# Linear attention in plain float32 on parts of TensorE, its keys and queries in bursts beside the feed-forward

## The chip, the cores and the metric

The kernel runs on one core of a Trainium2 chip. The time is that of one execution on the device in microseconds (us), lower is better. The core has a matrix engine (PE, which loads weights, PEld, and streams a moving operand against them), a vector engine (DVE), an activation engine (ACT), GpSimd (POOL), and a queue of transfers that SyncE (SP) issues. Each takes its own instructions in order; semaphores join them. Matmul results land in PSUM, eight banks of 2 KB per partition, and DVE or ACT must read a bank before it can be used again.

## The reference

Eight batches of eight heads, 576 tokens, head dimension 64, 128 features; then a feed-forward of 512 to 2048 to 512 over all 4608 tokens:

```python
def phi(x):
    proj = np.einsum('bhsd,df->bhsf', x, w_phi)
    proj = proj - np.max(np.abs(proj), axis=-1, keepdims=True)
    return np.concatenate([np.exp(proj), np.exp(-proj)], axis=-1)
q_p, k_p = (phi(q), phi(k))
kv = np.einsum('bhsf,bhsd->bhfd', k_p, v)
z = np.sum(k_p, axis=2)
num = np.einsum('bhsf,bhfd->bhsd', q_p, kv)
den = np.einsum('bhsf,bhf->bhs', q_p, z)[..., None] + 1e-06
x = num / den                      # heads side by side: 4608 x 512
h = x @ w_in
g = h * np.tanh(softplus(h))
out = g @ w_out
```

The weights of the feed-forward come as float64 and are brought to float32 on the chip. All else is float32.

## The kernel before

The feed-forward works on 18 chunks of 256 tokens. For each chunk `ff_in` (L352) makes 16 blocks of 128 hidden features, 12 matmuls of 128x128 by 256 columns each; `mish` (L367) applies the activation to two blocks; `ff_out` (L384) adds 6 matmuls of 512 columns a block into two PSUM tiles `o`. Both use float32r, a faster form of float32 on PE: every operand is a sum of a high and a low part (`gh` and `gl`, `xTh` and `xTl`, the two halves of a weight tile), and three products stand for one. `split_weight` (L116) turns 32 pieces of float64 words into such parts, with four operations on DVE, three on ACT and two on POOL a piece.

The keys are 72 units of 256 columns. `k_proj` (L203) calls `project` (L149): ACT and POOL split the raw keys, six float32r matmuls against a w_phi that holds two heads side by side give `pp_k`, DVE takes the largest magnitude (`m_k`, L146) and subtracts it (`d_k`, L165), ACT takes the two exponentials. `k_sum` (L210) adds `kvps` with the values stationary (66 columns: 64 values, a column of ones for the denominator, and one of zeros) and the 256 features as the moving operand, in plain float32. The result lies the wrong way round, is turned by `kvt` (L230), and goes out to DRAM and back.

A query unit is two heads of one chunk; there are four a chunk. `q_proj` (L252) splits and projects (`pp_q`, L177), `q_turn` (L256) transposes the result (`dt_q`), `q_exp` (L266) takes exponentials, once in float32 and once in float32r with the low part by POOL, `q_num` (L301) makes numerator and denominator in three float32r products with `kvs`, a split copy of kv; `q_den` (L326) sends the denominators through DRAM to spread them over the partitions, `q_out` (L340) divides.

The order comes from a table of due times (L405 to L456) in units of one feed-forward block: every call gets a time, they are sorted, and the framework's scheduler then places the instructions on the engines. All 72 key units have times below zero (`t0`, L429), 1.1 units apart, ahead of the first block; the query units of a chunk are four blocks apart during the chunk before. Weight pieces are spread over the same stretch.

Of the kernel before, what the change touches and what calls it, by code (L numbers as in the profile page):

```python
# [8 lines left out]
F32 = mybir.dt.float32  # L9
# [7 lines left out]
P = 128  # L17
# [4 lines left out]
VW = D + 2  # L22
# [5 lines left out]
NRAW, NE, NEH, NEL, NV, NKV = 3, 4, 2, 2, 2, 5  # L28
NHALF, NX, NRB, NXT, NG = 2, 2, 1, 3, 4

GP, GQ, GV = 2.2, 2.2, 1.5
GK, VLOAD = 2.7, 1.5
LOAD, WLOAD, KVLOAD = 4.0, 3.0, 3.0
Q0, Q1, QOUT, QL = -1.0, 4.0, 4.5, 0.5
QPOS, UPRE = 60, 1.1
W0, W1 = 4.0, 2.0
LAG, TAIL, TAILLAG = 4, 10, 2

KPLAIN, QPLAIN = 1, 1

NSPARE, WIN, MSPARE = 32, 4, 5
# [3 lines left out]
def attention_then_mish(ctx, tc, qT, kT, va, w_phi, w_in, w_out, out):  # L45
# [5 lines left out]
    dram = ctx.enter_context(tc.tile_pool(name="dram", bufs=4, space=bass.MemoryType.DRAM))  # L51
# [13 lines left out]
    def raw_tile(name):  # L65
        return work.tile([P, 2, 2 * P], F32, tag="raw", name=name, bufs=NRAW)

    def half_tile(name):
        return work.tile([P, 512], F32, tag="half", name=name, bufs=NHALF)


    wphi_raw = moe.tile([P, 2 * F], F32, tag="xTh", name="wphi_raw", bufs=NXT)
    nc.sync.dma_start(wphi_raw, w_phi[0])
    wphi_hi = moe.tile([P, 2 * F], F32R, tag="gh", name="wphi_hi", bufs=NG)
    wphi_lo = moe.tile([P, 2 * F], F32R, tag="gl", name="wphi_lo", bufs=NG)
    nc.vector.tensor_copy(wphi_hi, wphi_raw)
    nc.vector.tensor_sub(wphi_lo, wphi_raw, wphi_hi.bitcast(F32))
    wst_raw = moe.tile([P, 2 * F], F32, tag="xTl", name="wst_raw", bufs=NXT)
    nc.sync.dma_start(wst_raw, w_phi[1])
    wst = const.tile([P, 2 * F], F32R, tag="wst", name="wst")  # L80
    nc.vector.tensor_copy(wst, wst_raw)
    nc.vector.tensor_sub(wst[:D, F:], wst_raw[:D, F:], wst[:D, F:].bitcast(F32))
# [7 lines left out]
    spare = [f"w{kind}_{i}_{j}" for kind, i, j in pieces[-NSPARE:]]  # L90
    turn = 0
# [5 lines left out]
    def pair_tile(name):  # L97
        nonlocal turn
        if len(spare) >= MSPARE:
            turn += 1  # L100
            return slot_tile(spare[turn % min(WIN, len(spare))], F32, name)
        return work.tile([P, 2, 512], F32, tag="e", name=name, bufs=NE)

    piece = 0

    def load_weight(kind, i, j):
        nm = f"{kind}_{i}_{j}"
        if f"w{nm}" in spare:
            spare.remove(f"w{nm}")
        src = w_in[i * P:(i + 1) * P, j * 512:(j + 1) * 512] if kind == "in" else w_out[i * P:(i + 1) * P, :]  # L110
        slot = f"w{kind}_{i}_{j}"
        words = slot_tile(slot, U32, f"words_{nm}").rearrange("p a b -> p (a b)")
        nc.sync.dma_start(words, src.bitcast(U32))
        weight[kind, i, j] = words.rearrange("p (a b) -> p a b", b=2)

    def split_weight(kind, i, j):  # L116

        nonlocal piece
        nm = f"{kind}_{i}_{j}"
        slot = f"w{kind}_{i}_{j}"  # L120
        words = weight[kind, i, j]
        low, high = words[:, :, 0], words[:, :, 1]
        tag, bufs = ("u", 3) if piece % 5 < 3 else ("ee", 2)
        piece += 1
        w = moe.tile([P, 512], U32, tag=tag, name=f"w_{nm}", bufs=bufs)
        scale = moe.tile([P, 512], U32, tag="n", name=f"scale_{nm}")
# [9 lines left out]
        parts = slot_tile(slot, F32R, slot)  # L136
# [5 lines left out]
    def less_max(d, name):  # L142

        d3 = d.rearrange("p (n f) -> p n f", f=F)
        m = work.tile([P, 4], F32, tag="m", name=f"m_{name}", bufs=3)
        nc.vector.tensor_reduce(m, d3, axis=AX.X, op=ALU.max, apply_absolute_value=True)  # L146
        return d3, m.unsqueeze(2).broadcast_to([P, 4, F])

    def project(raw, plain, name):  # L149

        parts = ((raw, wphi_raw),)
        if not plain:
            hl = work.tile([P, 2, 2 * P], F32R, tag="hl", name=f"hl_{name}")
            hi, lo = hl[:, 0, :], hl[:, 1, :]
            nc.scalar.copy(hi, raw)  # L155
            nc.gpsimd.tensor_sub(lo, raw, hi.bitcast(F32))  # L156
            parts = ((hi, wphi_hi), (hi, wphi_lo), (lo, wphi_hi))
        ps = (ps_h if starting else ps_att).tile([P, 512], F32, tag="h" if starting else "att", name=f"pp_{name}")
        for i in range(2):
            for k, (x, w) in enumerate(parts):  # L160
                nc.tensor.matmul(ps[:, i * 2 * F:(i + 1) * 2 * F], x[:, i * P:(i + 1) * P], w,  # L161
                                 start=(k == 0), stop=(k == len(parts) - 1))
        d = pair_tile(f"d_{name}")
        p3, m = less_max(ps, name)
        nc.vector.tensor_tensor(d[:, 0, :].rearrange("p (n f) -> p n f", f=F), p3, m, op=ALU.subtract)  # L165
        return d

    def project_stacked(raw, name):

        x = work.tile([P, 2, 2 * P], F32R, tag="hl", name=f"hl_{name}")  # L170
        nc.scalar.copy(x, raw)  # L171
        nc.gpsimd.tensor_sub(x[D:], raw[D:], x[D:].bitcast(F32))  # L172
        d = pair_tile(f"d_{name}")
        for i in range(2):
            ps = ps_att.tile([P, 2, 2, F], F32, tag="att", name=f"pp{i}_{name}")
            for j in range(2):
                nc.tensor.matmul(ps[:, j], x[:, j, i * P:(i + 1) * P], wst, start=True, stop=True)  # L177
            di = d[:, 0, i * 2 * F:(i + 1) * 2 * F].rearrange("p (j f) -> p j f", f=F)
            nc.scalar.copy(di, ps[:, :, 1, :])
            nc.vector.tensor_tensor(di, ps[:, :, 0, :], di, op=ALU.add)  # L180
        d3, m = less_max(d[:, 0, :], name)
        nc.vector.tensor_tensor(d3, d3, m, op=ALU.subtract)
        return d


    kv, kv_dram = {}, {}
    k_live, k_raw, v_live, kv_ps = {}, {}, {}, {}

    def k_load(b, u):
        n = 9 * b + u  # L190
        if n % 2 == 0:
            k_raw[n // 2] = raw_tile(f"kraw_{n // 2}")
            nc.sync.dma_start(k_raw[n // 2], kT[n // 2])
        k_live[b, u] = k_raw[n // 2][:, n % 2, :]

    def v_load(b, u):
        for pair, first in ((0, 0), (1, 4), (2, 9), (3, 13)):
            if first // 2 == u:
                vt = work.tile([P, 5, 2, VW], F32, tag="v", name=f"v_{b}_{pair}", bufs=NV)
                nc.sync.dma_start(vt.rearrange("p t j w -> p (t j w)"), va[b * NHP + pair])  # L200
                v_live[b, pair] = vt

    def k_proj(b, u):  # L203
        nm = f"k_{b}_{u}"
        e = project(k_live.pop((b, u)), 9 * b + u < KPLAIN, nm)
        nc.scalar.activation(e[:, 1, :], e[:, 0, :], AF.Exp)
        nc.scalar.activation(e[:, 0, :], e[:, 0, :], AF.Exp, scale=-1.0)  # L207
        k_live[b, u] = e

    def k_sum(b, u):  # L210
        e = k_live.pop((b, u))
        for i in range(2):
            t = 2 * u + i
            for pair, first in ((0, 0), (1, 4), (2, 9), (3, 13)):
                slot = t - first
                if not 0 <= slot < 5:
                    continue
                if slot == 0:
                    pool, tag = (ps_o, "o") if starting else (ps_att, "att")
                    kv_ps[pair] = pool.tile([P, 2, 2, F], F32, tag=tag, name=f"kvps_{b}_{pair}")  # L220
                vt = v_live[b, pair]
                for j in range(2):
                    nc.tensor.matmul(kv_ps[pair][:VW, j], vt[:, slot, j, :], e[:, :, (2 * i + j) * F:(2 * i + j + 1) * F],  # L223
                                     start=(slot == 0 and j == 0), stop=(slot == 4), skip_group_check=True)
                if slot == 4:
                    kvT = half_tile(f"kvT_{b}_{pair}")
                    nc.scalar.copy(kvT[:VW], kv_ps.pop(pair)[:VW].rearrange("w j s f -> w (j s f)"))
                    ps = ps_att.tile([P, 512], F32, tag="att", name=f"kvt_{b}_{pair}")
                    for n in range(4):
                        nc.tensor.transpose(ps[:, n * VW:(n + 1) * VW], kvT[:VW, n * P:(n + 1) * P], ident[:VW, :VW])  # L230
                    t2 = work.tile([P, 4 * VW], F32, tag="kv", name=f"kvo_{b}_{pair}", bufs=NKV)
                    nc.vector.tensor_copy(t2, ps[:, :4 * VW])
                    kv_dram[b, pair] = dram.tile([P, 4 * VW], F32, tag=f"kvd_{b}_{pair}", name=f"kvd_{b}_{pair}", bufs=1)
                    nc.sync.dma_start(kv_dram[b, pair], t2)
                    del v_live[b, pair]
# [261 lines left out]
```

## Time and profile before

| what | value |
|---|---|
| median of 3 runs | 1229.3 us (1227.18 to 1231.24) |
| the profiled execution, its own time | 1229.93 us |
| its span | 1228.0 us |
| mean granted clock of PE | 0.996 |
| instructions | 21711, of them 8094 matmuls |
| HBM read, written | 69.40 MB, 13.91 MB |

The page gives busy times, and groups of instructions with "busy, mean ns of one | idle before". A matmul's own length holds its way through the array and is longer than its pitch, the distance from one start to the next, by which a row of them advances. The chain of waits, followed back from the last instruction, gives pitches: there a piece "x12" is the time in which twelve matmuls went by. The table by stage gives each engine's busy time in stretches of the span. The lines themselves stand in the prediction, beside the sums made from them.

### The profile page before, as it was taken

To read this page: it belongs to the slowest core of one execution; us is meant where nothing else is said; L and a number is where in the kernel's file an instruction comes from. 1 tells how busy PE (TensorE), PEld (TensorE's weight loads), DVE (VectorE), ACT (ScalarE), POOL (GpSimd) and SP (SyncE) were. 2 spreads that over 40 slices of the span, in tenths; PEclk is the share of its full clock that TensorE was granted. 3 is DMA by queue.
4 is the path that set the end of the run, shared out by engine and by line. 5 is a ranking of instruction groups with operands and counts; after the bars stand their busy time and mean duration, and the time that the engine had idled before them with its cause. 6 is when DMAs were issued, how large, how long until landed. Compare 5 with 4: busy or idle time off the path is not lost.

```text
span 1228.0 us, 21711 instructions
## 1 busy us (share of the span) xinstructions
PE 1199.2 (98%) x8094; PEld 1064.4 (87%) x8094; DVE 597.2 (49%) x987; ACT 895.2 (73%) x1704; POOL 594.9 (48%) x509
## 2 busy tenths in 40 slices
PE   8999998899999999999999999999999999999998
PEld 6776776688999899999999999999999999999997
DVE  6987887954443344334443444334343444344211
ACT  6887877788777767777777777777777777777531
POOL 3765665856544545454444544545454544544200
PEclk9999999899999999999999999999999999999999
DMA  5665657311111211110121111111111111010000
GB/s 194 206 187 176 200 159 229 99 57 36 53 44 40 61 31 51 38 53 27 49 65 36 44 28 56 31 53 27 57 61 32 44 40 53 27 36 14 25 24 18
DMA packets 62025, 84.87 MB, mean 69 GB/s; under 512 B 17632, under 2 KB 35808, under 8 KB 61920
## 3 DMA queue, kind: packets, MB, share of 16 engines
q1 hardware_dynamic: 61920, 83.49, 22.0%
q8 instruction: 63, 1.03, 0.3%
q14 instruction: 42, 0.34, 0.1%
HBM read 69.40 MB, written 13.91 MB: 68 GB/s over the span
## 4 chain that ended last, share of the span: by engine, by line
PE 81%; DVE 7%; DMA 5%; ACT 2%; issue 2%; POOL 1%; SPq 0%; POOLq 0%; DVEq 0%
PE h L364 33%; PE o L395 32%; PE num_q L313 8%; PE kvps L223 3%; PE pp_q L177 2%; PE dt_q L262 2%; DMA words_out<-w_out 2%; DMA words_in<-w_in 2%; DVE m_k L146 1%; DVE d_k L165 1%; PE pp_k L161 1%; DVE scale_in L133 1%; DVE scale_out L128 1%; DMA rb<-r 1%; DVE w_in L132 1%
## 5 line engine op out<-in xcount | busy, mean ns | idle before, releaser
L364 PE MATMUL h<-xTh,win 128*128 128x256 f32 x2304 | 466.3, 284 | 0.0
L381 DVE TENSOR_TENSOR gl<-u,gh 128x256 fp32r<-128x256 f32 x288 | 169.1, 613 | 479.6 <-ACT gh L380 476.5
L364 PEld LDWEIGHTS h<-xTh,win 128*128 128x128 f32 x2304 | 378.2, 190 | 9.4
L395 PE MATMUL o<-wout,gh 128*128 128x512 f32 x1152 | 364.5, 396 | 0.0
L364 PE MATMUL h<-xTl,win 128*128 128x256 f32 x1152 | 325.3, 283 | 0.0
L279 POOL TENSOR_TENSOR el_q<-d_q,eh_q 128x512 fp32r<-128x512 f32 x136 | 180.0, 1335 | 295.4 <-ACT eh_q L278 295.4
L364 PEld LDWEIGHTS h<-xTl,win 128*128 128x128 f32 x1152 | 219.0, 190 | 6.8
L395 PE MATMUL o<-wout,gl 128*128 128x512 f32 x576 | 224.8, 391 | 0.0
L395 PEld LDWEIGHTS o<-wout,gh 128*128 128x128 f32 x1152 | 198.4, 189 | 25.8
L223 PE MATMUL kvps<-d_k,v 128*66 128x256 f32 x640 | 151.9, 383 | 5.4 <-ACT d_k L207 4.4
L172 POOL TENSOR_TENSOR hl_q<-qraw,hl_q 64x512 fp32r<-64x512 f32 x68 | 88.5, 1301 | 105.5 <-ACT hl_q L171 90.2
L272 ACT ACTIVATE d_q<-dt_q 128x512 f32<-128x512 f32 x144 | 86.1, 601 | 71.6 <-PE dt_q L262 71.3
L395 PEld LDWEIGHTS o<-wout,gl 128*128 128x128 f32 x576 | 108.3, 188 | 23.8
L223 PEld LDWEIGHTS kvps<-d_k,v 128*66 128x66 f32 x640 | 86.0, 139 | 48.2 <-ACT d_k L207 6.7
L380 ACT CAST gh<-u 128x256 fp32r<-128x256 f32 x288 | 109.0, 406 | 20.5 <-PE o L395 11.9
L372 ACT ACTIVATE u<-h 128x512 f32<-128x512 f32 x144 | 86.1, 598 | 49.7 <-PE h L364 49.0
L313 PE MATMUL num_q<-eh_q,kvs 128*66 128x256 f32 (+3 forms) x736 | 107.9, 255 | 0.9 <-ACT eh_q L278 0.9
L298 POOL TENSOR_TENSOR kvs<-kv,kvs 128x264 fp32r<-128x264 f32 x92 | 81.4, 895 | 19.3 <-ACT kvs L297 13.7
L313 PE MATMUL num_q<-el_q,kvs 128*66 128x256 f32 (+3 forms) x368 | 88.9, 256 | 1.2 <-POOL el_q L279 1.2
L372 ACT ACT_TABLE_LOAD x69 | 88.5, 1283 | 1.2
L156 POOL TENSOR_TENSOR hl_k<-kraw,hl_k 128x256 fp32r<-128x256 f32 x71 | 60.5, 856 | 57.8 <-ACT hl_k L155 57.7
L161 PE MATMUL pp_k<-wphi_hi,hl_k 128*128 128x256 f32 x284 | 76.3, 331 | 10.9 <-DVE d_k L165 9.8
(74 smaller groups left out, 1694.9 us busy)
## 6 DMA issues: line engine op xcount, KB each, us to landing
qraw<-qT SPq DMA_DIRECT2D x136, 128.0 KB, 3.0
v<-va SPq DMA_DIRECT2D x32, 330.0 KB, 3.4
kraw<-kT SPq DMA_DIRECT2D x36, 256.0 KB, 3.5
rb<-r SPq DMA_DIRECT2D x72, 128.0 KB, 3.0
out<-osb SPq DMA_DIRECT2D x36, 256.0 KB, 2.1
words_in<-w_in SPq DMA_DIRECT2D x16, 512.0 KB, 4.4
words_out<-w_out SPq DMA_DIRECT2D x16, 512.0 KB, 4.1
kvd<-kvo SPq DMA_DIRECT2D x32, 132.0 KB, 1.8
```

Of the source, the lines that this page charges most:

```text
L161: nc.tensor.matmul(ps[:, i * 2 * F:(i + 1) * 2 * F], x[:, i * P:(i + 1) * P], w, start=(k == 0), stop=(k == len(parts) - 1))
L172: nc.gpsimd.tensor_sub(x[D:], raw[D:], x[D:].bitcast(F32))
L223: nc.tensor.matmul(kv_ps[pair][:VW, j], vt[:, slot, j, :], e[:, :, (2 * i + j) * F:(2 * i + j + 1) * F], start=(slot == 0 and j == 0), sto ...
L272: nc.scalar.activation(e, ps, AF.Exp, scale=2.0 * s - 1.0)
L279: nc.gpsimd.tensor_sub(el, e, eh.bitcast(F32))
L298: nc.gpsimd.tensor_sub(wl, w, wh.bitcast(F32))
L313: nc.tensor.matmul(ps[:VW, j, r0:r1], w[:, j, s, :], e[:, j * CH + r0:j * CH + r1], start=first, stop=(s == 1 and k == len(parts) - 1), sk ...
L364: nc.tensor.matmul(ps, w[:, wcol], x[:, cc % 2, :], start=(n == 0), stop=(n == 11))
L372: nc.scalar.activation(u, hv, AF.Mish)
L380: nc.scalar.copy(gh, u[:, f * CH:(f + 1) * CH])
L381: nc.vector.tensor_sub(gl, u[:, f * CH:(f + 1) * CH], gh.bitcast(F32))
L395: nc.tensor.matmul(ps, g[:, cols], w, start=(i == 0 and k == 0), stop=(i == NFT - 1 and k == 2))
```

## The change

The attention is in plain float32 throughout, and its matmuls use parts of the array.

- **Projections.** The raw tile has head j of a pair on partitions 64j to 64j+63. `project` (new L113) issues, for each 128 tokens, one matmul on rows 0 to 63 and one on rows 64 to 127, each of 128 features, into two different PSUM tiles. There are 576 of them, for keys and queries alike; nothing is split.
- **Sums.** In `halves` (new L133) phi is the stationary operand, 64 of its columns at a time, and the output goes to the matching half of the PSUM partitions; the moving operand is the 66 columns of the values, or of kv. Keys: 1280 such matmuls of 64 columns by 66; queries: 1152. kv comes out the right way round and stays in SBUF (`NKV` = 10 tiles); the 64-column halves also let one tile of queries straddle two batches.
- **Division.** The denominator now lies along partitions beside its numerator: DVE adds 1e-6, takes the reciprocal of 128x4 and multiplies (new L217 to L219). `x` is then transposed by PE (`xt`, new L227).
- **Order.** 36 key steps of 512 columns and 36 query steps (half a chunk, four heads) go together, key step n with query step n - 5 (`LEAD`). The first steps stand 2.4 units apart, the others 8, so that most keys fall beside the feed-forward. In each step the two projections stand together, and the exponentials come in two bursts of four. `table` (new L105) ties all exponentials and Mish calls into one order on ACT.

```diff
-NRAW, NE, NEH, NEL, NV, NKV = 3, 4, 2, 2, 2, 5
+NRAW, NE, NV, NKV = 4, 6, 3, 10
...
+NK, LEAD, USTART = B * NHP * S // 512, 5, 2.4
+E0, E1, GX = 0.27, 0.36, 1.2
...
+    def project(raw, name):
...
+        for n in range(4):
             for j in range(2):
+                rows = slice(j * D, (j + 1) * D)
+                nc.tensor.matmul(ps[j][:, n], raw[rows, n * P:(n + 1) * P], w_phi2[rows], start=True, stop=True)
...
+    def halves(ps, lhsT, rhs, start, stop):
+
+        for h in range(2):
+            rows = slice(h * D, (h + 1) * D)
+            nc.tensor.matmul(ps[rows], lhsT[:, rows], rhs[h], start=start, stop=stop, skip_group_check=True)
...
+                for j in range(2):
+                    for s in range(2):
+                        halves(ps[:, j, s], es[j][:, s, i * P:(i + 1) * P], (vt[:, slot, j, :],) * 2,
+                               start=(slot == j == s == 0), stop=(slot == 4))
...
+        for i in range(2):
+            ps = ps_att.tile([P, 2, 2, VW], F32, tag="att", name=f"num{i}_{c}_{g}")
+            for t in range(2):
+                r0 = (2 * c + t) * P
                 for j in range(2):
+                    for s in range(2):
+                        halves(ps[:, t, j], es[j][:, s, (2 * i + t) * P:(2 * i + t + 1) * P],
+                               [kv[(r0 + h * D) // S, 2 * g + i][:, j, s] for h in range(2)],
+                               start=(t == j == s == 0), stop=(s == 1))
...
+    steps = [(n - LEAD, n if n < NK else None, divmod(n - LEAD, 2) if 0 <= n - LEAD < 2 * NCH else None)
+             for n in range(LEAD + 2 * NCH)]
+    when = {n: 8.0 * n - 18.0 if n >= 2 else 8.0 * 2 - 18.0 - USTART * (2 - n) for n in range(-LEAD, 2 * NCH + 1)}
+    for n, key, query in steps:
+        t, t1 = when[n], when[n + 1]
+        d = t1 - t
...
+            at(t, k_proj, key)
...
+            at(t + 0.03, q_proj, *query)
...
+            at(t1 + 0.01, k_sum, key)
...
+            at(t1 + 0.02, q_num, *query)
+            at(t1 + GX, q_out, *query)
```

Two places show how the order changes. The first is DVE where the first low part of an activation (`gl` of chunk 0) is made, the mark of the feed-forward's start. Before, 326 instructions stand ahead of it, the last key unit (`m_k_8`, `d_k_8`) among them:

```order
L165 TENSOR_TENSOR d_k_7_2589<-pp_k_7_2582,m_k_7_2590 128x512
L232 COPY kvo_1_2572<-kvt_1_2567 128x264
L128 TENSOR_SCALAR scale_out_0_2790<-words_out_0_2707 128x512
L146 TENSOR_REDUCE m_k_8_2639<-pp_k_8_2631 128x4
L165 TENSOR_TENSOR d_k_8_2638<-pp_k_8_2631,m_k_8_2639 128x512
L127 TENSOR_SCALAR w_out_0_2789<-words_out_0_2707 128x512
L133 SCALAR_TENSOR_TENSOR scale_out_0_2790<-words_out_0_2707,scale_out_0_2790 128x512
L132 SCALAR_TENSOR_TENSOR w_out_0_2789<-words_out_0_2707,w_out_0_2789 128x512
L381 TENSOR_TENSOR gl_0_0_2779<-u_0_2776,gh_0_0_2778 128x256
```

Now 161 stand ahead of it. `xTl_1` is the last input that chunk 0 needs, the projection of `e_q_0` belongs to chunk 1:

```order
L219 TENSOR_TENSOR x_1_936<-num_0_1_958,r_0_1_975 128x256
L127 TENSOR_REDUCE m_q_0_990<-pp_q_0_979 128x4
L127 TENSOR_REDUCE m_q_0_994<-pp_q_0_980 128x4
L128 TENSOR_TENSOR e_q_0_989<-pp_q_0_979,m_q_0_990 128x512
L128 TENSOR_TENSOR e_q_0_993<-pp_q_0_980,m_q_0_994 128x512
L231 TENSOR_TENSOR xTl_1_1029<-xt_1_1023,xTh_1_1028 128x512
L88 TENSOR_SCALAR w_out_0_1106<-words_out_0_1009 128x512
L88 TENSOR_SCALAR w_out_0_1137<-words_out_0_1032 128x512
L93 SCALAR_TENSOR_TENSOR w_out_0_1106<-words_out_0_1009,w_out_0_1106 128x512
L262 TENSOR_TENSOR gl_0_0_1099<-u_0_1096,gh_0_0_1098 128x256
```

The reductions and subtractions of 29 of the 36 key steps (58 of the 72 units before) have moved behind this place, into the chunks.

The second is PE inside a chunk. Before, a query unit stands between two blocks of `h`: two pairs of projections, then numerators in float32r (`eh`, `el` are the parts of the exponentials, `kvs` the split kv; a row that straddles two batches has 64 and 192 columns):

```order
L364 MATMUL h_2_9337<-xTh_1_9256,win_0_475 128x256
L177 MATMUL pp_q_2_9354<-wst,hl_q_2_9350 128x256 x2
L177 MATMUL pp_q_2_9359<-wst,hl_q_2_9350 128x256 x2
L313 MATMUL num_q_1_9370<-eh_q_1_9294,kvs_1_4_9325 66x64 x2
L313 MATMUL num_q_1_9370<-el_q_1_9295,kvs_1_4_9325 66x64
...
L313 MATMUL num_q_1_9370<-eh_q_1_9294,kvs_1_5_9328 66x192 x2
```

Now a burst stands there: the key sums of the step before (`kvps`, for two head pairs), the numerators of the query step, then the next query projections, one head's before an `o` block and the other's behind it:

```order
L137 MATMUL kvps_5125<-v_5008,e_k_5108 64x66 x4
L137 MATMUL kvps_5476<-v_5335,e_k_5104 64x66 x4
...
L137 MATMUL num_7_0_5510<-kv_3780,e_q_0_5215 64x66 x4
L137 MATMUL num_7_0_5531<-kv_4131,e_q_0_5211 64x66 x4
L137 MATMUL num_7_0_5531<-kv_4131,e_q_0_5215 64x66 x4
L122 MATMUL pp_q_1_5552<-w_phi_83,qraw_1_5320 128x128 x4
L276 MATMUL o_0_5399<-wout_0_346,gh_6_1_5351 128x512 x2
...
L122 MATMUL pp_q_1_5553<-w_phi_83,qraw_1_5320 128x128 x4
```

The key sums, which stood ahead of the feed-forward, have moved between its blocks, about 36 a step, with 32 numerators.

More of the change, by code (lines that the diff above doesn't have):

```diff
@@ L63, in attention_then_mish @@
     nc.vector.memset(exp_bias, -7.0 * 2 ** 30)
[L65 to L82, printed above, removed]
+    w_phi2 = const.tile([P, F], F32, tag="w_phi", name="w_phi2")
+    nc.sync.dma_start(w_phi2, w_phi)
     pieces = [("in", i, 0) for i in range(NCC)]
@@ L140, in split_weight @@
         nc.gpsimd.tensor_sub(lo, w, hi.bitcast(F32))
[L142 to L175, printed above, removed]
-            for j in range(2):
[L177 to L183, printed above, removed]
@@ L186, in attention_then_mish @@
[L186 to L201, printed above, removed]
@@ L203, in k_proj @@
[L203 to L217, printed above, removed]
+    last = None
@@ new lines, in table @@
+    def table(act):
+        nonlocal last
+        if last is not None:
+            tc.add_manual_dep(act.ins, last.name, mybir.DependencyInfo(mybir.DependencyClass.NoSync, mybir.DependencyReason.DATA),
+                              reason="table")
+        last = act.ins
+    def project(raw, name):
+        ps = []
+        for j in range(2):
+            pool, tag = (ps_h, "h") if starting else (ps_att, "att")
+            ps.append(pool.tile([P, 4, F], F32, tag=tag, name=f"pp{j}_{name}"))
+        for n in range(4):
+            for j in range(2):
+                rows = slice(j * D, (j + 1) * D)
+                nc.tensor.matmul(ps[j][:, n], raw[rows, n * P:(n + 1) * P], w_phi2[rows], start=True, stop=True)
+        es = []
+        for j in range(2):
+            e = work.tile([P, 2, 512], F32, tag="e", name=f"e{j}_{name}", bufs=NE)
+            m = work.tile([P, 4], F32, tag="m", name=f"m{j}_{name}", bufs=4)
+            nc.vector.tensor_reduce(m, ps[j], axis=AX.X, op=ALU.max, apply_absolute_value=True)
+            nc.vector.tensor_tensor(e[:, 0, :].rearrange("p (n f) -> p n f", f=F), ps[j],
+                                    m.unsqueeze(2).broadcast_to([P, 4, F]), op=ALU.subtract)
+            es.append(e)
+        return es
@@ new lines, in v_load, with k_proj, k_exp @@
+    def v_load(n):
+        for t in range(4 * n, 4 * n + 4):
+            for p, slot in pairs_of(t):
+                if slot == 0:
+                    vt = work.tile([P, 5, 2, VW], F32, tag="v", name=f"v_{p}", bufs=NV)
+                    nc.sync.dma_start(vt.rearrange("p t j w -> p (t j w)"), va[p])
+                    v_live[p] = vt
+    def k_proj(n):
+        k_live[n] = project(k_live.pop(n), f"k_{n}")
+    def k_exp(n, j):
+        e = k_live[n][j]
+        table(nc.scalar.activation(e[:, 1, :], e[:, 0, :], AF.Exp))
+        table(nc.scalar.activation(e[:, 0, :], e[:, 0, :], AF.Exp, scale=-1.0))
@@ L227, in k_sum @@
[L227 to L232, printed above, removed]
@@ L342, in q_out @@
+    def q_out(c, g):
+        x = x_live.pop((c, g))
+        ps = ps_att.tile([P, 2, CH], F32, tag="att", name=f"xt_{c}_{g}")
+        for i in range(2):
+            for t in range(2):
+                nc.tensor.transpose(ps[:, i, t * P:(t + 1) * P], x[:, i, t], ident)
         hi = moe.tile([P, 2, CH], F32R, tag="xTh", name=f"xTh_{c}_{g}", bufs=NXT)
         lo = moe.tile([P, 2, CH], F32R, tag="xTl", name=f"xTl_{c}_{g}", bufs=NXT)
-        nc.gpsimd.tensor_mul(x, x, rb)
-        nc.scalar.copy(hi, x)
@@ L396, in ff_out @@
             if f == NFT - 1:
-                o = half_tile(f"osb_{c}_{tt}")
+                o = work.tile([P, DM], F32, tag="half", name=f"osb_{c}_{tt}", bufs=NHALF)
                 if c == NCH - 1 and tt:
```

245 lines of the change are left out of this document (67 added, 178 removed).

## The prediction

> **What bounds the kernel now.** I read the page first: the busy time of each engine.
>
> ```profile
> PE 1199.2 (98%) x8094; PEld 1064.4 (87%) x8094; DVE 597.2 (49%) x987; ACT 895.2 (73%) x1704; POOL 594.9 (48%) x509
> ```
>
> TensorE (PE) is busy 98% of the span, the others three quarters or less. But a matmul is counted until its result has drained, so 98% can hide slack. The table by stage shows it; its columns are the stretch, its length, and the busy time of PE, weight loads, VectorE (DVE), ScalarE (ACT) and GpSimd (POOL).
>
> ```profile
> 0.00:50.00 50.00, 44.11 (x247) 33.83 (x248) 36.53 (x64) 35.99 (x69) 24.57 (x31) 1.00 0.61 198
> 50.00:100.00 50.00, 46.87 (x278) 35.08 (x277) 41.55 (x69) 39.45 (x78) 32.38 (x30) 1.00 0.64 195
> 100.00:150.00 50.00, 47.67 (x283) 35.27 (x282) 40.27 (x69) 40.17 (x79) 31.22 (x30) 1.00 0.57 185
> 150.00:200.00 50.00, 48.16 (x278) 35.88 (x277) 40.84 (x68) 38.61 (x76) 27.57 (x27) 1.00 0.58 175
> 200.00:250.00 50.00, 40.46 (x234) 30.54 (x233) 44.16 (x63) 40.42 (x77) 42.44 (x34) 0.93 0.46 143
> 300.00:400.00 100.00, 100.00 (x708) 92.28 (x707) 39.27 (x67) 74.82 (x141) 47.21 (x39) 1.00 0.15 45
> 1170.00:1228.00 58.00, 53.94 (x333) 48.27 (x331) 8.28 (x19) 14.70 (x31) 1.30 (x1) 0.98 0.05 19
> ```
>
> There are two stages. Up to about 250 us PE issues 5 matmuls per us (247 in 50) although it looks busy, and DVE, with 203.35 of 250 us, is the fullest in-order engine: this stage is bound by DVE and by the waits between engines. From 300 us on PE issues 7 per us without a gap. The chain of waits (start, length, what) shows one chunk of that second stage:
>
> ```profile
> 638.87 2.75 PE o L395 x12
> ...
> 650.52 0.47 PE pp_q L177 x4
> 650.99 1.41 PE num_q L313 x12
> 652.40 1.43 PE h L364 x12
> 653.83 1.39 PE o L395 x6
> ...
> 658.04 0.44 PE dt_q L262 x4
> ...
> 693.22 2.75 PE o L395 x12
> ```
>
> One chunk lasts 693.22 - 638.87 = 54.35 us, all of it PE. The pitches add up to it: 16 times (1.43 + 1.39) is 45.1, and four query units of 0.47 + 1.41 + 0.44 are 9.3, together 54.4. So here the sum of PE pitches is the time, and whatever the other engines do is hidden. 18 chunks are 979 us. After the last matmuls
>
> ```profile
> 1214.40 9.56 PE o L395 x42
> ```
>
> come 1228.0 - 1223.96 = 4.0 us of copy and store. That leaves 1228 - 979 - 4 = 245 us for the first stage. The sums below are made against the profiled execution: 1229.93 us, span 1228.0, so 1.9 around the span; the median shown, 1229.3, is the same to 0.1%.
>
> **The change, stage by stage. The start.** Now 72 key units stand ahead of the first feed-forward on DVE; afterwards seven key steps (of twice a unit's size), three query steps and some 23 weight pieces. From the order I count what DVE does up to xTl_1, the last input of chunk 0: 22 reductions and 22 subtractions of 128x512, 92 weight operations, 6 key-value copies, 4 normalisations, 2 xTl. Their prices, as busy, mean ns:
>
> ```profile
> L165 DVE TENSOR_TENSOR d_k<-pp_k,m_k 128x512 f32<-128x512 f32 x72 | 49.1, 684 | 1.1
> L146 DVE TENSOR_REDUCE m_k<-pp_k 128x4 f32<-128x512 f32 x72 | 49.0, 681 | 10.3 <-PE pp_k L161 10.2
> L133 DVE SCALAR_TENSOR_TENSOR scale_out<-words_out,scale_out 128x512 uint32<-128x512 uint32 x16 | 15.9, 1005 | 0.0
> L133 DVE SCALAR_TENSOR_TENSOR scale_in<-words_in,scale_in 128x512 uint32<-128x512 uint32 x16 | 14.9, 935 | 0.0
> L232 DVE COPY kvo<-kvt 128x264 f32<-128x264 f32 x32 | 13.5, 422 | 2.1 <-PE kvt L230 2.1
> L132 DVE SCALAR_TENSOR_TENSOR w_out<-words_out,w_out 128x512 f32<-128x512 uint32 x16 | 13.1, 820 | 3.0 <-ACT w_out L130 3.0
> L132 DVE SCALAR_TENSOR_TENSOR w_in<-words_in,w_in 128x512 f32<-128x512 uint32 x16 | 12.5, 778 | 1.1 <-ACT w_in L130 1.1
> L128 DVE TENSOR_SCALAR scale_out<-words_out 128x512 uint32<-128x512 uint32 x16 | 11.9, 768 | 0.0
> L127 DVE TENSOR_SCALAR w_out<-words_out 128x512 uint32<-128x512 uint32 x16 | 10.8, 677 | 11.3 <-DMA words_out<-w_out 11.1
> L127 DVE TENSOR_SCALAR w_in<-words_in 128x512 uint32<-128x512 uint32 x16 | 9.8, 613 | 10.1 <-DMA words_in<-w_in 9.8
> L128 DVE TENSOR_SCALAR scale_in<-words_in 128x512 uint32<-128x512 uint32 x16 | 9.2, 589 | 0.0
> ```
>
> 44 x 0.683 = 30.0; 22 x 0.645 + 24 x 0.679 + 22 x 0.799 + 24 x 0.970 = 71.5; 6 x 0.42 = 2.5; four normalisations of at most two copies' worth (0.84) are 3.3; xTl 1.4: 109 us. DVE was busy 203.35/250 = 0.81 in the stage now, with the same mix, so the start takes 109/0.81 = **134 us**. The best window (0.88) gives 123, the worst (0.73) 149. The transfers come close to it: SP's queue now has all 32 weight pieces ahead of the first query data, with keys and values 19 MB, 97 us at the 198 GB/s of the first window; DVE reaches the first query reduction after 78 us of work, 78/0.81 = 96. A slower queue would show there, and the 149 covers it. The other nine pieces (28 us of DVE) fall beside chunk 0, whose last weights are wanted after twelve blocks of 2.82, 34 us; up to 10 us could be lost there.
>
> **The feed-forward** is untouched: 288 blocks x (1.43 + 1.39) = **812 us**.
>
> **Attention on PE behind the start.** Of the order's rows, 272 transposes of the queries, 136 of x, 488 projections and 2120 sums (kvps and num) stand behind xTl_1's place. The transposes are dt's: 0.44/4 = 0.11, so 408 x 0.11 = 44.9. For the rest I need the pitch of plain float32. Timeline and chain rows (start, length), then groups with mean ns:
>
> ```profile
> 188.73 0.86 PE pp_q L161 x4
> ```
> ```profile
> 233.91 0.41 PE L230 MATMUL kvt<-ident,kvT 66*128 66x66 f32 x4
> 403.14 0.28 PE L313 MATMUL num_q<-eh_q,kvs 128*66 128x128 f32 x2
> 403.20 0.14 PEld L313 LDWEIGHTS num_q<-el_q,kvs 128*66 128x66 f32 x1
> 403.26 0.22 PE L313 MATMUL num_q<-el_q,kvs 128*66 128x128 f32 x1
> ```
> ```profile
> L230 PE MATMUL kvt<-ident,kvT 66*128 66x66 f32 x128 | 13.3, 226 | 0.3
> L223 PEld LDWEIGHTS kvps<-d_k,v 128*66 128x66 f32 x640 | 86.0, 139 | 48.2 <-ACT d_k L207 6.7 <-DMA v<-va 1.2 <-issue 1.1
> L161 PEld LDWEIGHTS pp_q<-wphi_raw,qraw 128*128 128x128 f32 x16 | 2.9, 190 | 0.8 <-PE dt_q L262 0.4
> ```
>
> 256 moving float32 columns cost 0.86/4 = 0.215 us, 128 (dt) 0.11; 66 columns (kvt: four in 0.41, the last of 0.226) (0.41 - 0.226)/3 = 0.061. So one sum is 0.060 and one projection 0.11 if they run one after the other. The new code issues them as neighbours on different columns (sums) or rows (projections) of the array; if two lie fully side by side they cost half, 0.030 and 0.055. No row of this trace has two parts of the array at work, so these are the two ends. I take the lower, for this reason: neither of a pair needs the other's result, cells or PSUM partitions, and the stages above show nothing else that paces PE at 0.060 (weight loads lie beside matmuls: the load at 403.20 runs inside the matmuls that start at 403.14). It gives 2120 x 0.030 = 63.6 for the sums, whose halves always alternate. Of the projections only 273 alternate between the rows in the order; the other 215, nearly all of queries, stand in runs of four on the same rows with feed-forward blocks between, and pay in full: 273 x 0.055 + 215 x 0.11 = 38.7. With the transposes **147 us**; all one after the other it is 2120 x 0.060 + 488 x 0.11 + 44.9 = 226.
>
> **Changes of shape.** The order goes 241 times between whole array, rows and columns, seven times a step. The nearest rows price this at nothing (at 658.04 plain float32 follows float32r without a gap); from the other side a pipeline that must drain costs what a matmul lasts beyond its pitch, 0.22 - 0.06 = 0.16, or 39 us. I take half, **19**. The Trainium skill, TensorEngine Tiling (Array Packing), section Tiling Modes, Key Properties, speaks on both points: separate tiles run loads and matmuls in parallel, but a change of tiling mode drains TensorE. By the first the sums cost 63.6, by the second the changes 39; no row here shows either.
>
> **What it costs at nothing.** ACT loses the casts of k, q, eh and kv and the copies of d and x (1704 instructions before, 1024 after) and keeps its exponentials and about as many table loads; POOL loses all but the weights; the round trips of kv and 1/den through DRAM go. All this lay beside the 54.4 us chunks, so its going saves nothing but the start's contention. New on DVE in a chunk: the reductions and subtractions of two key steps (8 x 0.683 = 5.5 us) in place of the longer query chain; DVE has 60 of 100 us free there. New waits: in each burst PE's next projection waits for a PSUM bank that DVE empties 4 x 0.683 = 2.7 us after pp_k; twelve h matmuls (1.43) and 70 sums (2.1) stand between, so little is left, 0 to 1 us a step; I take 0.2, **7 us**. Behind a waiting projection the whole PE queue stands.
>
> **Sum**: 134 + 812 + 147 + 19 + 7 + 4 + 2 = **1125 us**.
>
> **Rivals.** *One after the other*: the halves do not overlap, the change does not do what it says. Then 1125 + 226 - 147 = **1204**. For it: every pitch in this trace belongs to a single stream. Against it: nothing shows what would force it.
>
> *Loads of column halves cannot run ahead* (slower). Both halves use the same 128 rows, and if a half's weights load only when the array is still, each sum pays load and matmul. From 66 to 128 columns a load grows by 190 - 139 = 51 ns, 0.82 ns a column, 53 ns for 64. A sum is then 0.060 + 0.053 = 0.113, and the time 1125 + 2120 x 0.083 = **1301**. It turns slower than now from 0.030 + (1230 - 1125)/2120 = 0.080 a sum. Against it: the load at 403.20 overlaps a matmul on the same rows. The Trainium skill, TensorE: Matmul & The Clock Gate, Part 3, The mechanism, has this as a rule: loads overlap matmuls in flight only where the row group differs. The trace disagrees for the whole array, where all loads share the rows; for halves no row decides.
>
> *Bursts wait for PSUM banks*: with four attention banks and a shorter run of sums, PE stands 1.5 us more a step, 34 x 1.5 = 51: **1176**. For it: one bank is always held by kvps. Against it: the 3.5 us of PE work above.
>
> **How the numbers follow.** Forecast 0.55, one after the other 0.27, loads not ahead 0.12, banks 0.06. The forecast's own range is 1095 (start 123, no price for the changes of shape) to 1160 (start 149, changes at 39); with the rivals at 1176 and 1204 I put 1085 to 1215, which leaves out the slower rival and the edges. A measurement of this kernel tells 0.3% (3.7 us) from no change: faster 0.85 (all but the slower rival and a little of the second), same 0.02, slower 0.13.
>
> **What would show it.** The first gl near 135 us, not 250; a chunk of 54 to 56 us; sums at 0.030 pitch, alternating projections at 0.055; gaps below 0.2 us at the changes; PE in the chunks waiting for nobody. Wrong would be sums at 0.06 or above, or PE waiting on DVE in each burst.

## The result, and the profile after

The changed kernel takes **1250.7 us** (median of four runs, 1249.8 to 1252.7) where the kernel before takes 1229.1 in the same comparison: a ratio of 1.018, 95% interval 1.016 to 1.020. It is 1.8% slower; the forecast was 1125 us, with a range of 1085 to 1215. The profiled execution took 1249.8 us, its span is 1247.8.

The busy times first (engine, busy us, share of the span, instructions):

```profile
PE 1174.2 (94%) x11632; PEld 1050.6 (84%) x11632; DVE 499.2 (40%) x991; ACT 616.0 (49%) x1023; POOL 91.0 (7%) x70
```

The other engines did what the change let expect: POOL is down to 70 instructions, ACT from 73% to 49%. PE is the surprise: 11632 instructions in the trace, while the program has 8624 matmuls, transposes included. The groups of PE show where the others come from (pattern, count, busy us, mean ns of one, idle before):

```profile
L137 PE MATMUL kvps<-v,e_k 128*64 128x66 f32 x2560 | 91.0, 233 | 1.6 <-ACT e_k L166 1.6
L137 PE MATMUL num<-kv,e_q 128*64 128x66 f32 x2304 | 77.3, 224 | 6.7 <-ACT e_q L202 5.0 <-DVE e_k L128 1.8
L122 PE MATMUL pp_q<-w_phi,qraw 64*128 64x128 f32 x576 | 74.3, 293 | 7.1 <-issue 3.9 <-DVE e_k L128 3.0
L122 PE MATMUL pp_k<-w_phi,kraw 64*128 64x128 f32 x576 | 64.6, 315 | 32.8 <-issue 16.3 <-DVE e_k L128 12.2 <-DMA kraw<-kT 4.1
L200 PE MATMUL dt<-ident,e_q 128*128 128x128 f32 x288 | 44.3, 277 | 17.6 <-DVE e_q L128 17.6
```

The program issues 1280 matmuls into kvps, 1152 into num, 288 into pp_q and 288 into pp_k: the trace has exactly twice as many of each, and exactly as many transposes (dt, 288) as the program. The 1280 + 1152 + 576 matmuls counted once more are the whole difference of 3008. **A plain float32 matmul is two PE instructions, each with a weight load of its own; a transpose is one.** One of the two is called a pass below. The kernel before had this in its trace too: the loads of kvps that the prediction quotes are x640 where its program has 320, those of pp_q<-wphi_raw x16 for 8. So the 8094 "matmuls" in the table of the kernel before are PE instructions; its program has 7766.

The table by stage (columns as in the prediction; the third number from the end is the granted clock of PE):

```profile
0.00:50.00 50.00, 21.75 (x272) 19.83 (x272) 41.66 (x57) 26.28 (x42) 25.59 (x24) 0.83 0.96 373
50.00:100.00 50.00, 22.27 (x216) 19.41 (x216) 49.97 (x63) 26.54 (x42) 33.23 (x24) 0.57 0.21 70
300.00:400.00 100.00, 100.00 (x1011) 89.77 (x1010) 33.61 (x74) 48.29 (x81) 0.00 (x0) 1.00 0.11 33
```

The start went as foreseen, bound by VectorE (49.97 of 50 us), and it ends early: the rows of the last input of chunk 0 and of the first gl say when (for a tile, its count, min/median/max ns, first and last start):

```profile
L231 DVE TENSOR_TENSOR xTl<-xt,xTh x2: 681/686/692, 118.8 to 128.0; 128x512 fp32r<-128x512 f32 x2
L262 DVE TENSOR_TENSOR gl<-u,gh x6: 389/422/1502, 134.9 to 158.6; 128x256 fp32r<-128x256 f32 x6
```

xTl_1 is there at 128.7 us (forecast 134), the first gl starts at 134.9. From 300 us on PE is without a gap and at the full granted clock, as before, but with 10 instructions per us instead of 7; the lower clocks in the table stand in the start. The chain of waits shows a step, half a chunk:

```profile
600.14 1.08 PE pp_k L122 x14
601.23 1.56 PE h L249 x12
602.79 2.49 PE kvps L137 x80
605.28 1.87 PE num L137 x64
607.15 1.08 PE pp_q L122 x8
608.24 1.59 PE o L276 x6
609.83 0.12 PE h L249
609.94 1.08 PE pp_q L122 x8
611.03 1.50 PE h L249 x11
612.52 0.44 PE xt L227 x4
612.96 1.40 PE o L276 x6
614.36 1.42 PE h L249 x12
615.77 0.44 PE dt L200 x4
...
632.11 1.09 PE pp_k L122 x16
633.21 1.61 PE h L249 x12
634.82 2.02 PE kvps L137 x64
636.84 1.87 PE num L137 x64
```

Three things can be read here. 64 instructions of num are 32 sums: 1.87/32 = **0.058 us a sum**, not 0.030. Eight instructions of pp_q are four projections on the same rows, 1.08 us; sixteen of pp_k are eight that alternate, 1.09. And a block behind a burst is longer than its like further on: 1.61 against 1.42 (h), 1.59 against 1.40 (o), so **a change of shape costs about 0.19**. From the first h matmul of a chunk to that of the next it is 64.1 us; before it was 54.4. Fourteen such chunks eat the 111 us that the start gained (first h matmul at 127.7 us instead of 238.5), and more.

### The profile page after: what moved, and what is told of

Its sections match the earlier page's. It is cut to its first block, busy times and chain, and to the rows that moved or that the text cites. A ratio compares the mean times of both kernels' runs of the same rounds, so it can differ in the third digit from the quotient of the medians.

```text
span 1247.8 us, 26586 instructions
## 1 busy us (share of the span) xinstructions
PE 1174.2 (94%) x11632; PEld 1050.6 (84%) x11632; DVE 499.2 (40%) x991; ACT 616.0 (49%) x1023; POOL 91.0 (7%) x70
## 4 chain that ended last, share of the span: by engine, by line
PE 89%; DVE 7%; ACT 1%; issue 1%; DMA 0%; POOL 0%; SPq 0%; DVEq 0%; ACTq 0%; POOLq 0%
PE o L276 33%; PE h L249 33%; PE kvps L137 5%; PE pp_q L122 5%; PE num L137 5%; PE pp_k L122 3%; PE dt L200 2%; PE xt L227 1%; DVE scale_in L94 1%; DVE w_in L93 1%; DVE scale_in L89 1%; DVE scale_out L89 1%; DVE w_out L93 1%; DVE m_k L127 1%; DVE w_in L88 1%
## 5 line engine op out<-in xcount | busy, mean ns | idle before, releaser
L262 DVE TENSOR_TENSOR gl<-u,gh 128x256 fp32r<-128x256 f32 x288 | 118.4, 439 | 548.6 <-ACT gh L261 546.2
L261 ACT CAST gh<-u 128x256 fp32r<-128x256 f32 x288 | 110.9, 409 | 38.7 <-PE o L276 19.6
L122 PE MATMUL pp_k<-w_phi,kraw 64*128 64x128 f32 x576 | 64.6, 315 | 32.8 <-issue 16.3
L122 PEld LDWEIGHTS pp_k<-w_phi,kraw 64*128 64x128 f32 x576 | 52.8, 212 | 50.7 <-issue 49.4
L137 PE MATMUL kvps<-v,e_k 128*64 128x66 f32 x2560 | 91.0, 233 | 1.6 <-ACT e_k L166 1.6
L137 PEld LDWEIGHTS kvps<-v,e_k 128*64 128x64 f32 x2560 | 85.1, 146 | 7.4 <-ACT e_k L166 2.3
L202 ACT ACTIVATE e_q<-dt 128x512 f32<-128x512 f32 x144 | 78.2, 595 | 17.0 <-PE dt L200 16.5
L137 PE MATMUL num<-kv,e_q 128*64 128x66 f32 x2304 | 77.3, 224 | 6.7 <-ACT e_q L202 5.0
L122 PE MATMUL pp_q<-w_phi,qraw 64*128 64x128 f32 x576 | 74.3, 293 | 7.1 <-issue 3.9
L137 PEld LDWEIGHTS num<-kv,e_q 128*64 128x64 f32 x2304 | 73.1, 140 | 8.6 <-ACT e_q L202 5.2
L122 PEld LDWEIGHTS pp_q<-w_phi,qraw 64*128 64x128 f32 x576 | 62.1, 195 | 16.8 <-issue 14.1
```

What stands on the lines that cost most here:

```text
L122: nc.tensor.matmul(ps[j][:, n], raw[rows, n * P:(n + 1) * P], w_phi2[rows], start=True, stop=True)
L137: nc.tensor.matmul(ps[rows], lhsT[:, rows], rhs[h], start=start, stop=stop, skip_group_check=True)
L202: table(nc.scalar.activation(e[:, s, :], ps, AF.Exp, scale=2.0 * s - 1.0))
L261: nc.scalar.copy(gh, u[:, f * CH:(f + 1) * CH])
L262: nc.vector.tensor_sub(gl, u[:, f * CH:(f + 1) * CH], gh.bitcast(F32))
```

## The experiments

My theory after the result: each plain float32 matmul is two passes; the halves do run side by side, so that a pair of passes takes 0.058 us; a change of shape costs 0.19. The rivals: one pass each with the halves one after the other; changes free; the loss in waits for banks. The runs e1, e4, e5, e8 and e9 were executed once each, the others four times.

**e1: key sums on the whole array.** The other sums and all projections stay.

```diff
-halves(ps[:, j, s], es[j][:, s, i * P:(i + 1) * P], (vt[:, slot, j, :],) * 2, ...)
+nc.tensor.matmul(ps[:, j, s], es[j][:, s, i * P:(i + 1) * P], vt[:, slot, j, :], ...)
```

> Theory: each plain float32 matmul is two PE instructions, each with its own weight load, and two halves run side by side: a pair of passes every 0.058 us, so two half sums cost 2 x 0.058 = 0.117 us. With the key sums on the whole array the pair becomes one matmul of 128 columns, two passes of about 0.107 us (what four projections on the same rows show), 0.215 us. Some 600 such pairs stand behind the start, so 600 x 0.098 = +59 us against the changed kernel's 1250: about 1309 us; kvps shows 1280 PE instructions in place of 2560, and 16 whole sums of a step take 3.4 us in the chain instead of 1.9. Rival (the halves run one after the other, each in one pass of 0.058): joining two halves on the whole array takes as long as one of them, so the time falls by 600 x 0.058 = 35 us to 1215. Second rival (the halves give nothing and cost nothing): no change, 1250.

Measured: 1318.0 us. The group of the key sums, and the chain:

```profile
L178 PE MATMUL kvps<-v,e_k 128*128 128x66 f32 x1280 | 174.3, 303 | 1.2 <-ACT e_k L166 1.2
```
```profile
675.86 1.61 PE h L249 x12
677.47 3.52 PE kvps L178 x32
680.99 2.02 PE num L137 x64
```

1280 instructions are 640 matmuls, and 16 of them take 3.52 us, 0.22 each, where their two halves take 0.117. A chunk grows from 64.1 to 67.9 us, and the start, which has key sums too, ends 17 us later. The halves do not run one after the other. That 1318 is near the forecast of 1309 is partly luck: behind the start the trace has 2064 instructions of kvps in the changed kernel, 516 pairs and not 600, which alone give 53 us, and the 17 us of the start were not in the forecast. The change of shape has moved from kvps to num (2.02 for 1.87), as it must.

**e2: projections alternate.** A chain without waits (`behind`) keeps the eight matmuls of a unit in the order of the code.

```diff
+        prev = None
         for n in range(4):
-            for j in range(2):
+            for j in (0, 1):
...
-                nc.tensor.matmul(ps[j][:, n], ...)
+                mm = nc.tensor.matmul(ps[j][:, n], ...)
+                if prev is not None:
+                    behind(mm.ins, prev)
+                prev = mm.ins
```

> Only the order of the projections is changed: the eight of a unit alternate between the two row halves. Theory: 215 projections that stood in runs on the same rows fall from 0.22 to 0.11 us each, -24 us; the number of changes of shape stays (239 for 241): 1226 us, about the kernel before (1229). A run of eight pp_q matmuls (16 PE instructions) takes 1.08 us in the chain, as pp_k does, instead of 2.16. Rival (the lost time is waits for PSUM banks or for other engines, not the work of the array): no gain, 1250, since the banks and the work of DVE and ACT stay.

**e3: the same, gathered.**

```diff
-            at(t, k_proj, key)
+            at(t - (1.5 if d > 5 else 0), k_proj, key)
-            at(t + 0.03, q_proj, *query)
+            at(t + (1.1 if d > 5 else 0.03), q_proj, *query)
```

> As e2, with the projections of keys issued 1.5 blocks earlier and those of queries 1.1 blocks later, which leaves each group of eight in one piece: 196 changes of shape behind the start instead of 239, about 1.3 fewer a step. Theory (a change costs about 0.19 us of PE): 43 x 0.19 = 8 us less than e2: 1218, and 1% faster than the kernel before. Rival (a change is free, as my sum's lower end had it): as e2, 1226. Rival (banks): the later query projections find their banks free and PE's waits go, which the table of waits would show as time of pp_k and pp_q behind DVE.

Measured: e2 1225.4 us (ratio to before 0.996, interval 0.994 to 0.997), e3 1210.8 us (0.984, 0.982 to 0.986). Chains of e2, then of e3:

```profile
655.59 0.42 PE pp_q L128 x2
656.00 1.60 PE o L285 x6
657.60 0.82 PE h L258 x7
658.43 1.09 PE pp_q L128 x14
659.51 0.79 PE h L258 x5
```
```profile
646.90 1.59 PE o L285 x6
648.50 1.41 PE h L258 x12
649.91 1.09 PE pp_q L128 x16
651.00 0.59 PE xt L236 x4
```

e2 came out at its forecast (1226), though in part by luck: of the 23 us between the two profiles 16 come from the full chunks (64.1 to 62.8 us each), where 24 were expected, and 7 from a start and a first chunk each 3.5 us shorter, which the forecast did not have. In its chain one projection goes ahead alone, thirteen matmuls before the others (I take it that in the scheduled order its partner's bank comes free only then): it takes 0.42 us, and leaves the other seven without one partner. e3 has all eight in one piece of 1.09 us. Over a full chunk, what is beyond the bare pitches (h 0.1175, o 0.233, transposes 0.11, sums 0.029 and projections 0.0555 an instruction) adds up to 3.7 us at 16 changes of shape in e2, and to 2.2 at 12 in e3. The difference is the 1.5 us by which the chunk falls, 62.8 to 61.3. Half of it is four changes, half the lone projections (a group of seven lies 0.31 us above its bare pitches, a group of eight 0.20); I had counted the latter at nothing, so e3 gained 14.6 us instead of 8. In the full chunks no row shows PE waiting for a bank, or for anything, in either.

**e5: more changes.** e3 with the key sums of a step in four bursts.

```diff
-            at(t1 + 0.01, k_sum, key)
+            for i in range(4):
+                at(t1 + 0.01 + 0.5 * i, k_sum, key, i)
```

> As e3, but the key sums of a step are issued in four bursts of eight or sixteen half a block apart, with feed-forward matmuls between: 347 changes of shape behind the start instead of 196, and the same matmuls. Theory (a change costs 0.15 to 0.2 us of PE, 0.19 in the mean): 151 x 0.19 = +29 us over e3's 1211: 1240 us, and every feed-forward block that follows such a burst shows 1.6 instead of 1.4 us in the chain of waits. Rival (a change is free, and e3 gained on e2 only because its lone projections got their partners): 34 lone projections x 0.2 us are 7 of the 14.6 us, the rest by chance; e5 then stays at 1211.

Measured: 1233.9 us. The chain:

```profile
653.82 0.62 PE kvps L146 x16
654.43 1.87 PE num L146 x64
656.31 1.59 PE o L285 x6
657.90 0.62 PE kvps L146 x16
658.52 1.61 PE h L258 x12
660.13 1.09 PE kvps L146 x32
```

Sixteen instructions are 0.47 bare and take 0.62 when they follow another shape; the block behind takes 1.61. In a full chunk ten more changes (22 for 12) cost 1.7 us, 0.17 each: 61.3 against 63.0. The whole is 23 us for the 151 changes of the order where the forecast said 29; the start ended 2.3 us earlier than e3's, so behind it the changes cost 25 us, again 0.17 each. That is less than 0.19 since the new changes enter the column halves (0.15) or leave them (0.19 to 0.20). A change is not free.

**e4 and e6: sums in one pass.** The exponentials, the values and kv are rounded to bfloat16; e6 has e3's order as well.

```diff
+            es.append((e, work.tile([P, 2, 512], BF16, tag="eb", ...)))
...
+                    v_live[p] = work.tile([P, 5, 2, VW], BF16, tag="vb", ...)
+                    nc.gpsimd.tensor_copy(v_live[p], vt)
...
-work.tile([P, 2, 2, VW], F32, tag="kv", ...)
+work.tile([P, 2, 2, VW], BF16, tag="kv", ...)
```

> The exponentials, the values and kv are written as bfloat16 and the sums run on those (their precision is left out; the projections and transposes stay float32); POOL copies the values. Theory: a bfloat16 matmul is one PE instruction, so kvps shows 1280 and num 1152 instead of 2560 and 2304, and a pair of halves costs 0.058 us instead of 0.117 as long as the load of 64 columns (0.053) sets the pace, or less if it loads faster: 1060 pairs x 0.058 = -62 us, and the order has 29 more changes of shape, +6: about 1194 us, lower if loads are faster. Rival (a float32 sum is one pass of 0.060 and halves run one after the other): as many instructions as before and no more than the difference of rates, and if the 66 moving columns set the pace the time stays at 1250.

> e4 (sums in bfloat16, their precision left out) with e3's order of the projections. Theory: the terms add: of e4's projections 151 stood on the same rows, -151 x 0.11 = -17 us, and 25 changes of shape go (245 for 270), -5 us: 1148 - 22 = 1126 us, 8% under the kernel before. Rival (with so little left on PE another engine is the bound, DVE or ACT): the gain is smaller than 10 us and PE shows waits in the chunks.

Measured: e4 1147.9 us, e6 1136.4 us (0.924, 0.922 to 0.926). Groups and chain of e4:

```profile
L138 PE MATMUL kvps<-vb,eb_k 128*64 128x66 bf16 x1280 | 32.5, 206 | 14.0 <-ACT eb_k L168 7.1 <-POOL vb L160 6.3 <-DVE kv L184 0.6
L138 PE MATMUL num<-kv,eb_q 128*64 128x66 bf16 x1152 | 30.2, 198 | 4.5 <-DVE e_k L129 4.2 <-ACT eb_q L204 0.3
```
```profile
639.55 0.63 PE kvps L138 x32
...
669.09 0.76 PE kvps L138 x40
```

The counts halve, as the theory has it: one instruction a matmul. The pass is shorter too, which I had not expected: eight more instructions, four pairs, take 0.13 us, so a pair of passes is 0.033 instead of 0.058. A pair of bfloat16 sums thus costs 0.033 where one in float32 costs 0.117. e4 lands 46 us under its forecast: the shorter pass explains 27 (1060 pairs x 0.025), a start 18 us shorter with a first chunk 5.5 us longer another 12, and the last 7 are not assigned. e6 gained 11.5 us over e4 instead of 22: its chunk fell by only 0.9 us (57.7 to 56.8), since in its order a lone query projection still goes ahead of the other seven. Chain of e6:

```profile
609.85 0.42 PE pp_q L129 x2
610.70 1.09 PE pp_q L129 x14
```

Its rival, another engine as the bound, does not hold: from 300 to 1100 us PE waits for nothing in e4 or e6.

**e7: the weights later.**

```diff
-W0, W1 = 2.0, 9.0
+W0, W1 = 2.0, 12.0
```

> e3 with the weight pieces spread until block 12 instead of block 9; two pieces fewer stand before the last input of chunk 0 on VectorE. Theory (the end of chunk 0 is set by the whole of VectorE's work up to its last weight, so what the start gains, chunk 0 waits): the first feed-forward block 4 to 6 us earlier, the time within 3 us of e3's 1211. Rival (the start alone counts, and chunk 0 loses its time to something else): -6 us, 1205.

Measured: 1209.3 us (0.983, 0.982 to 0.985), 1.5 us under e3, which was measured at another time. The first feed-forward matmul comes 2.7 us earlier (the forecast said 4 to 6), and the first chunk is 0.6 longer, 71.3 against 70.7. So chunk 0 gave back little of what the start gained, and the theory behind this run is not borne out; the time is within 3 us of e3's because the start gained little. What chunk 0 loses against the later ones, 10 us here and 7 in the changed kernel, is not had by putting two pieces off. The trace shows where PE stood: it waits 9.2 us for VectorE and ACT in e7's chunk 0, and 5.7 us in the changed kernel's.

**e8: halves apart.** Of each four sums first the lower halves, then the upper.

```diff
         for h in range(2):
             rows = slice(h * D, (h + 1) * D)
-            nc.tensor.matmul(ps[rows], lhsT[:, rows], rhs[h], ...)
+            for ps, lhsT, rhs, start, stop in sums:
+                mm = nc.tensor.matmul(ps[rows], lhsT[:, rows], rhs[h], ...)
```

> The changed kernel with another order of the sums alone: of each four sums first the four on the lower column half, then the four on the upper, so that neighbours stand on the same columns; the same instructions, 237 changes of shape for 241. Theory (neighbours on different columns run side by side, a pass takes 0.058 us whether alone or in a pair): of eight passes of a group only the last can overlap the next group's first, so a sum costs 0.10 to 0.117 us instead of 0.058: +93 to +124 us over 1250, 1343 to 1374 us, and 64 instructions of num take 3.3 to 3.7 us in the chain instead of 1.87. Rival (halves run one after the other, each pass in half of 0.058): the order means nothing, 1250.

**e9: wider key sums.**

```diff
-(vt[:, slot, j, :],) * 2
+(vt[:, slot].rearrange("p j w -> p (j w)")[:, 32 * j:32 * j + 100],) * 2
```

> The changed kernel with 100 moving columns in each key sum instead of 66 (the other 34 are the other head's values and are not used); loads, counts and order stay. It asks what paces a pass at 0.058 us. If it is the 66 moving columns (0.86 ns each, as 128 in 0.111 say): 616 pairs x 2 passes x 34 x 0.86 ns = +36 us over 1250, 1286 us, and 80 instructions of kvps take 3.7 us in the chain instead of 2.49. If it is the load of 64 columns (0.82 ns each, 0.053): a pass takes 0.086 all the same once 100 columns are longer than the load, so the two are told apart by the size: below 66 columns' share the load hides the first few, and the pass grows from 0.058 by 0.028 or less. If a pass does not grow at all, a load and a fixed cost set it, and the time stays at 1250.

Measured: e8 1290.2 us, e9 1276.1 us. Chain of e8, then of e9:

```profile
656.71 2.46 PE kvps L144 x61
659.35 2.33 PE num L144 x59
```
```profile
614.19 3.58 PE kvps L137 x80
617.77 1.87 PE num L137 x64
```

e8 is slower, so the order of the halves matters and the serial rival falls; but it lost 40 us, not 93 to 124, and 6 of them in the start. The 64 instructions of num (59 records) take 2.33 us: sixteen passes in 0.58, ten intervals of 0.058, where eight are needed side by side and sixteen alone. The starts in the trace show it: of eight passes three begin within 6 ns of another, where the order of the program puts only one in eight beside a pass on the other half; the rest follow some 57 ns apart, so a pass alone takes as long as a pair. I read this as PE reaching further ahead than the one pass that I allowed it; the records do not name the half, so which passes pair up is not shown. In e9 the key sums take 3.58 us instead of 2.49 for 34 columns more: 1.09/40 = 27 ns a pass, 0.80 ns a column. With the 516 pairs of the trace (the expectation had 616) that is 28 us; the time grew by 25. So the moving columns set the pace of the halves; in e1, where as many columns move but 128 are loaded, a pass took 0.11 us, and there the load did.

## Why the prediction was wrong

The step that failed is "For the rest I need the pitch of plain float32", and in it the price of one matmul; that the halves overlap was right. The changes of shape were under-sized besides.

- **The price of a sum and of a projection: half of what it is.** I divided stretches of the chain by their counts (0.86/4) and set the counts of the *program* against the result. But the counts of the chain are PE instructions: the four of 0.86 us were two matmuls. For 66 columns I took kvt, which is a transpose and one pass (x128 for 128). A half sum costs 0.058 in its pair, not 0.030: 2120 x 0.0584 = 124 us for 63.6. The projections are 273 x 0.111 + 215 x 0.22 = 78 us for 38.7. Together +99 us. The rows were there: kvps x640 and pp_q x16, for 320 and 8 matmuls of the program.
- **Side by side: right.** Pairs take the time of one (e1, e2, e8). The forecast time of *one after the other*, 1204, is nearer the result, but for another reason: two sums of two passes each, side by side, take as long as two sums of one pass each, one after the other. The rival *loads of column halves cannot run ahead* had the right sign with a wrong mechanism: the loads do run ahead, for a pass of 0.058 us has no room for a load of 64 columns (0.053 by the prediction) and 66 moving columns at 0.80 ns (0.053) one after the other, and at 0.058 a sum is under that rival's turning point of 0.080. That point was worked out for the sums alone, with all else at its forecast; projections and changes of shape went past it.
- **Changes of shape: mis-sized.** 19 us, with 39 as the bound. 0.19 x 241 = 46 us, +27. The bound took the tail of one matmul (0.16), and I halved it; entering a shape costs 0.15 to 0.20, and leaving it as much again, and both are among the 241. The Trainium skill, TensorEngine Tiling (Array Packing), section Key Properties, says that a change of tiling mode drains TensorE; e5 agrees in that each change costs time, 0.17 us there, while no run here shows that a drain is the reason.
- **Start: right.** 128.7 us for 134: VectorE worked 112.0 us up to there, where the prediction counted 109, and was busy 0.87 of the time, for 0.81. **Feed-forward**: 288 x (1.41 + 1.40) = 809 for 812. **Transposes**: 0.44 for four, as taken.
- **Banks: 7 us that did not come.** In the full chunks the rows add up without a wait; a single matmul that goes ahead of its group is, as I read it, what the banks cost, as a change of shape.
- **Chunk 0**: 70.9 us where the next ones take 64.1, 7 us of the 10 that the text allowed and the sum left out. It has two parts. PE waits 5.7 us, most of it at 142 to 151 us while VectorE works on weight pieces. Then, from 149 to 166 us, its granted clock is 0.50, and the rows of that stretch are longer than their like later on (1.40, 1.61):

```profile
151.45 2.93 PE o L276 x6
161.95 2.56 PE h L249 x12
```

Over the stretch from 151.4 to 164.0 us the rows come to some 6 us more than their like, by my estimate. Against this, chunk 0 has 24 matmuls of `o` fewer (5.6 us), as `ff_out` runs four blocks behind.

With these: 128.7 + 809 + 124 + 78 + 44.9 + 46 + 7 + 6 = 1244 of 1250; the last 6 are not assigned.

The Trainium skill, FP8 and Floating Point Precision, section TensorE Precision Notes, counts true FP32 as four passes through the array. By the feed-forward's float32r, 1.41/(12 x 256) = 0.46 ns a column, an estimate from that is 66 x 4 x 0.46 = 0.121 us a matmul; the trace agrees with the cost on the column halves (0.117) but shows two instructions, and on the whole array (e1) the same 66 columns took 0.22.

Against the kernel before, e3 and e7 (plain float32 throughout) are 1.6% and 1.7% faster, e2 0.4%, and e4 and e6, whose sums are rounded to bfloat16, 7% and 8%.

## What to carry to other kernels

Before a pitch from the trace is multiplied by a count, put the trace's count of that operation beside the program's: where they differ, the price is that of a part. Take the price of an operation from the same operation and type, not from a transpose of the same shape. Where the array is used in parts, keep the partners adjacent and the groups whole: here a lone projection and the change back cost 0.61 us where it takes 0.11 in its group, and a burst of sixteen passes pays 0.34 us of changes for 0.47 of work.

## What the runs showed of the hardware

- A plain float32 matmul is two PE instructions with a load each, a transpose in float32 one. With 64 columns loaded, 66 moving columns take 0.058 us a pass (0.80 ns for each further column, e9), 0.117 in all, against 0.033 in bfloat16 (one instruction, e4).
- Column halves and row halves run side by side, with starts 6 to 7 ns apart; a pass takes about as long as the longer of its load and its moving columns (0.058 with 64 loaded and 66 moving, 0.086 with 64 and 100, 0.11 with 128 and 66).
- Halves that are not adjacent in the program still overlap in part (e8: ten intervals for sixteen passes).
- A change between the whole array and its parts, or between row and column parts, costs 0.15 to 0.20 us each way: 0.15 into column halves, 0.20 into row halves, 0.19 to 0.20 back to the whole array after a burst.
